# One output transfer per tile, a first tile of x by itself, and a new order of work

## The chip, the cores and the metric

The kernel runs on one core of a Trainium2 chip. The metric is the device time of one execution in microseconds (us); the median of three runs of the kernel before is 215.65 us (214.74 to 216.35). The core has five engines with an instruction stream each: PE (TensorE, matmuls; its weight loads are shown as PEld), DVE (VectorE), ACT (ScalarE), POOL (GpSimd) and SP (SyncE, which here only issues DMA transfers, in order). The transfers themselves are carried out by 16 DMA engines.

## The reference

For x of 2048 rows by 576 columns the result is the sum of three things:

```python
xn  = layernorm(x)                                  # over the 576 columns, eps 1e-5
A   = irfft2(rfft2(xn) * (w_r + 1j * w_i))          # over rows and columns
q   = einsum("nd,dhc->nhc", x, w_q)                 # 32 heads, c = 2 * 128
s1  = einsum("nhd,ed->nhe", q[..., :128], k1)       # 8 keys; s2 with k2
i1, i2 = argmax(s1), argmax(s2)                     # one of 8 each, top_e = 8 * i1 + i2
g   = softmax(one value) = 1
act = gelu(einsum("nd,nhd->nh", x, u[top_e]))       # tanh form
B   = einsum("nh,nhd->nd", g * act, v[top_e])       # 64 rows of u and v
out = x + A + B
```

## The kernel before

The rows are split into 16 tiles of 128. The work goes through five stages, which overlap.

1. Head. `ln` takes the mean and variance of each tile of x (DVE `BN_STATS` and `BN_AGGR`, or two ACT passes for the tiles in `SA`), and from them the factor `rr` of a row. `folds` adds and subtracts a tile's columns in mirrored pairs (`t`, then `F`, which the profile calls `A`), scales a 128x128 matrix by the rows' factors (`Rs`), and lays out the 33 middle columns (`yl`). `dft128` multiplies: two matmuls `Rs,yl` and four `Rs,A` per tile. The results of all 16 tiles go to `AB` and `ABL`. Statistics are done for groups of tiles: 2, 2, 4, 4 and 4, and the loads of x are cut the same way (`LOADS`).
2. Key fold. `fold_part` multiplies w_q (32 transfers of 576 KB) with the key differences `KP` (matmuls `w,KP`). These depend on no tile of x and are placed between other PE work.
3. Spectrum. For 16 groups g: `d_fwd` (matmuls `c,ABL` and `c,AB`; the first one needs all 16 tiles of the head), `s_fwd`, `s_mul`, `s_inv`.
4. Routing. `scores`, `route` and `combine` for 8 pairs of tiles.
5. Output. For each tile t, `d_inv(t)` and `fin(t, y)` (before: L1142). `fin` adds 16 matmuls of 64x64 weights into one PSUM pair, then one DVE `SCALAR_TENSOR_TENSOR` multiplies by a scale and adds x in place, into the tile `XN` (128 partitions by 2 by 288 columns: the partitions are 2 column halves c by 64 rows n, then 2 row halves h). Two transfers follow, one per column half:

```python
os = out.rearrange("(n h t) (c d) -> t c n h d", h=2, t=16, c=2)
for c in range(2):
    Q.dma_start(os[t, c], x[64 * c:64 * c + 64])
```

Each of the 32 transfers moves 144 KB from 64 partitions by 2 by 288 numbers to 128 rows by 288 numbers of the result in DRAM (the n and h steps merge into one step of 128): 128 pieces of 1152 bytes that are contiguous in DRAM.

Nothing is issued as it is written. A planner (`_Plan`) records every operation, gives it a cost (`cost`), merges runs of matmuls, and lays the operations out in time with a list of ranks (`RANK`, one number per operation) as priorities; instructions are then issued in that order on every engine. So each engine runs its stream in a fixed order that `RANK` and the costs determine, and waits for semaphores where data come from another engine. All recorded instructions have the line of the planner's loop (L542 before, L540 after). SP issues loads and outputs from one stream; all loads stand ahead of the outputs in it. The transfers use eight semaphores in turn, so a transfer waits until the eighth one before it has landed.

Of the kernel before, what the change touches and what calls it, by code (L numbers as in the profile page):

```python
# [14 lines left out]
AF = mybir.ActivationFunctionType  # L15
# [17 lines left out]
def _consts():  # L33
# [166 lines left out]
)  # L200
# [93 lines left out]
class _Plan:  # L294
# [41 lines left out]
    def add(self, eng, fn, m, args, kw):  # L336
# [7 lines left out]
        if AF.Gelu_apprx_tanh in args and not self.asked:  # L344
            self.asked, c = True, c + 1283.0
# [932 lines left out]
```

## Time and profile before

| | us |
|---|---|
| median of 3 runs | 215.65 (214.74 to 216.35) |
| profiled execution | 215.94, its span 214.2 |
| PE busy | 191.7 (89%) |
| DVE busy | 178.3 (83%) |
| ACT busy | 129.8 (61%) |
| POOL busy | 112.9 (53%) |
| mean granted TensorE clock | 0.987 |
| first matmul, last chain piece of PE until | 10.92, 208.13 |
| first output transfer issued | 180.81 |

The span runs from the first to the last instruction; the 1.7 us between the span and the profiled execution's own time lie around it. In the rows of the profile a group is named by what it writes and reads ("banks" is PSUM, `XN` the tiles of x and of the result, `out_dram` the result in DRAM). "us to landing" is from a transfer's issue to the moment its last data count as arrived. In rows on DMA, "share" is the busy time of packets as a share of 16 engines over the window; a packet is one contiguous piece.

### The profile page before, as it was taken

The numbers are of one execution on the slowest core, as the hardware profiler recorded it, in microseconds if no ns is written. First come the engines' busy times: TensorE is split into PE (matmuls) and PEld (weight loads), VectorE is DVE, ScalarE is ACT, GpSimd is POOL, SyncE is SP. The second block draws the span as 40 slices with busy tenths as digits, with TensorE's granted clock in tenths as the row PEclk, the third lists the DMA queues.
The fourth block names the chain that finished last, engine by engine and source line by source line (L and its number), as shares of the span: only waits on it lengthen the run. The fifth ranks groups of instructions, "written<-read, shape, count | busy, mean of one in ns | idle before, by whom it ended". The sixth has DMA issues, their size and how long they took to land.

```text
span 214.2 us, 6027 instructions
## 1 busy us (share of the span) xinstructions
PE 191.7 (89%) x2324; PEld 131.4 (61%) x2324; DVE 178.3 (83%) x426; ACT 129.8 (61%) x304; POOL 112.9 (53%) x153
## 2 busy tenths in 40 slices
PE   0093999989999999999999999999999999999980
PEld 0082877757856765674648464476465777878850
DVE  1999899941694956992999999999999999999880
ACT  2279699888948792984845964996454531222310
POOL 4356464612419840492523663879565147758750
PEclk9999799999999999999999999999999999999998
DMA  6999999999999999998543433102000000655566
GB/s 202 392 413 422 396 312 313 415 409 410 384 384 387 411 410 381 424 411 352 142 123 95 153 112 95 55 3 77 0 5 0 3 0 5 167 139 139 123 161 164
DMA packets 17020, 48.12 MB, mean 225 GB/s; under 512 B 2144, under 2 KB 8544, under 8 KB 16224
## 3 DMA queue, kind: packets, MB, share of 16 engines
q1 hardware_dynamic: 16992, 47.74, 62.7%
q8 instruction: 18, 0.29, 0.6%
q14 instruction: 10, 0.08, 0.1%
HBM read 43.01 MB, written 4.72 MB: 223 GB/s over the span
## 4 chain that ended last, share of the span: by engine, by line
PE 54%; DVE 32%; issue 5%; ACT 2%; POOL 2%; DMA 2%; DVEq 0%; POOLq 0%
PE banks L542 54%; DVE t L542 8%; DVE MT L542 5%; DVE A L542 4%; DVE st L542 3%; DVE w L542 2%; DVE AB L542 2%; DMA XN<-in_x_dram 2%; DVE ABL L542 2%; POOL t L542 2%; DVE mx L542 1%; DVE mm__96 L542 1%; DVE rr L542 1%; ACT yl L542 1%; POOL y L542 1%
## 5 line engine op out<-in xcount | busy, mean ns | idle before, releaser
L542 PE MATMUL banks<-MU,xT 128*128 128x512 f16 x192 | 45.2, 379 | 0.0
L542 PE MATMUL banks<-c,AB 128*128 128x145 f16 (+2 forms) x320 | 37.7, 251 | 0.4 <-DVE AB L542 0.4
L542 PEld LDWEIGHTS <-xT 128*128 128x128 f16 x224 | 20.9, 98 | 23.7 <-issue 0.4
L542 POOL TENSOR_TENSOR y<-t,t 128x289 f32<-128x289 f32 x32 | 23.2, 744 | 21.3 <-DVE t L542 19.1
L542 POOL TENSOR_TENSOR A<-t 128x289 f32<-128x289 f32 (+2 forms) x42 | 26.5, 649 | 14.7 <-PE banks L542 5.6
L542 DVE SCALAR_TENSOR_TENSOR t<-banks,wx,Wt 128x578 f32<-128x578 f32 x32 | 24.4, 811 | 4.4 <-ACT A L542 2.8
L542 POOL TENSOR_TENSOR yh<-y,yh 128x578 f16<-128x578 f32 x16 | 20.8, 1309 | 10.2 <-ACT yh L542 6.8
L542 PE MATMUL banks<-Rs,yl 128*99 128x128 f32 x64 | 11.2, 319 | 15.0 <-ACT yl L542 14.7
L542 POOL TENSOR_TENSOR xT<-xf,xT 128x640 f16<-128x640 f32 x10 | 14.2, 1428 | 17.8 <-ACT xf L542 11.0
L542 ACT ACTIVATE AB<-banks 128x512 f32<-128x512 f32 (+1 forms) x32 | 18.7, 591 | 3.8 <-PE banks L542 3.7
L542 PE MATMUL banks<-w,KP 128*32 128x288 f32 x256 | 20.3, 415 | 0.2 <-DMA w<-in_wq_dram 0.2
L542 ACT ACTIVATE yh<-banks 128x290 f32<-128x290 f32 (+1 forms) x16 | 7.3, 458 | 20.2 <-PE banks L542 13.5
L542 PEld LDWEIGHTS banks<-Rs,yl 128*99 128x99 f32 x64 | 9.0, 195 | 16.7 <-ACT yl L542 15.1
L542 PE MATMUL banks<-c,ABL 99*128 99x289 f16 (+1 forms) x64 | 19.1, 298 | 0.0
L542 POOL TENSOR_TENSOR t<-XN 128x289 f32<-128x289 f32 x14 | 13.1, 942 | 10.9 <-DVE A L542 5.3
L542 PEld LDWEIGHTS banks<-c,AB 128*128 128x128 f32 x128 | 18.0, 190 | 1.3 <-DVE AB L542 0.6
L542 PEld LDWEIGHTS banks<-Rs,A 128*128 128x128 f32 x128 | 16.7, 207 | 3.3 <-issue 2.3
L542 PE MATMUL banks<-Rs,A 128*128 128x128 f32 x128 | 18.3, 295 | 0.0
L542 DVE TENSOR_REDUCE MT<-w 128x128 bf16<-128x896 bf16 (+1 forms) x16 | 18.2, 1138 | 0.0
L542 PE MATMUL banks<-A,s 64*64 64x289 f32 x256 | 17.5, 410 | 0.0
L542 PEld LDWEIGHTS <-AB 128*128 128x128 f16 x192 | 17.2, 147 | 0.1
L542 DVE TENSOR_TENSOR ABL<-banks,ABL 33x256 f16<-33x256 f32 x32 | 13.0, 410 | 5.0 <-ACT ABL L542 4.7
(129 smaller groups left out, 408.4 us busy)
## 6 DMA issues: line engine op xcount, KB each, us to landing
w<-in_wq_dram SPq DMA_DIRECT2D x32, 576.0 KB, 6.9
xf<-in_xT_dram SPq DMA_DIRECT2D x16, 320.0 KB, 5.1
Wt<-in_W_dram SPq DMA_DIRECT2D x8, 578.0 KB, 6.6
out_dram<-XN SPq DMA_DIRECT2D x32, 144.0 KB, 2.5
XN<-in_x_dram SPq DMA_DIRECT2D x3, 1154.0 KB, 9.2
s<-in_s_dram SPq DMA_DIRECT2D x16, 192.0 KB, 4.4
XN<-in_xd_dram SPq DMA_DIRECT2D x2, 1152.0 KB, 9.0
XN<-in_xd_dram SPq DMA_DIRECT2D x1, 2304.0 KB, 10.6
```

Source lines behind the costliest of these rows:

```text
L542: ins = fn(*[x.place() if isinstance(x, _Ps) else x for x in args], **{k: x.place() if isinstance(x, _Ps) else x for k, x in kw.items()}).ins
```

## The change

Five things change.

- The first load of x covers tile 0 alone, the second tile 1, then tiles 2 and 3; the statistics are grouped 1, 1, 2, 4, 4 and 4.
- `fin` issues one transfer per tile, for both column halves. It moves 288 KB from 128 partitions by 2 by 288 numbers to 2 (column halves) by 128 (rows) by 288 numbers of DRAM.
- For tile 15, `fin` works on columns 0 to 143 and 144 to 287 of each half apart: 16 matmuls, one `SCALAR_TENSOR_TENSOR` and one transfer for each part, with 2 by 128 pieces of 576 bytes.
- Five costs or rules of the planner change (a factor for matmuls with 64x64 weights, POOL costs, the table load's cost, the rule for the port that DVE and POOL share, and the time for a change of the PE's tile shape).
- `RANK` is replaced, so the order on every engine is new.

```diff
-    464, 1220, 901, 1223, 1261, 1268, 1219, 1221, 391, 444, 431, 691, 894, 879, 874, 922, 835, 890, 883, 839,
...
+    1181, 1226, 1183, 1212, 1228, 1233, 1232, 1227, 1225, 897, 443, 1139, 442, 597, 1021, 564, 562, 563, 603,
...
-                return c * q[0] * q[1] / 16384 * (0.935 if q == [64, 128] else 1.065), 230.0
+                return c * q[0] * q[1] / 16384 * (0.935 if q == [64, 128] else 1.037), 230.0
...
-            return 45 + 1.15 * n, 75.0
+            return (45 if not ins else 120 if n > 16 else 200) + 1.15 * n, 75.0
...
-        if AF.Gelu_apprx_tanh in args and not self.asked:
+        if AF.Gelu_apprx_tanh in args and not self.asked and not self.extra:
...
-            len(sb) > 1 or m in ("tensor_copy", "tensor_scalar") and len(sb) == 1 == len(ins))
+            len(sb) > 1 or m in ("tensor_copy", "tensor_scalar") and len(sb) == 1)
...
-                    t0 = max(t0, free[e] + CHANGE)
+                    t0 = max(t0, free[e] + (120.0 if o.shape[0] == [128, 128] else 90.0))
...
-                if t0 - free[e] > 2500.0:
+                if t0 - free[e] > 2500.0 or not warm:
...
-    LOADS = ((0, 2), (2, 2), (4, 4), (8, 4), (12, 4))
-    Q.dma_start(XN[:, 0:2], xs[:, 0:2])
+    LOADS = ((0, 1), (1, 1), (2, 2), (4, 4), (8, 4), (12, 4))
+    Q.dma_start(XN[:, 0:1], xs[:, 0:1])
...
     def fin(t, y):
+        x = XD[:, t]
+        if t == 15:
+            for n, z in enumerate((slice(0, 144), slice(144, 288))):
+                p = PS("bc"[n])
+                for k in range(4):
+                    for h in range(2):
+                        hs = slice(64 * h, 64 * h + 64)
+                        for c in range(2):
+                            cs, ds = slice(64 * c, 64 * c + 64), slice(288 * c + z.start, 288 * c + z.stop)
+                            w, m = ((RT[hs], y[hs, ds]) if k == 0 else
+                                    (CAT[hs, t, 64 * (k // 3):64 * (k // 3) + 64], vS[hs, k % 2 ^ 1, ds]))
+                            P.matmul(p[cs, h, z], w, m, start=(k == 0), stop=(k == 3), tile_position=(64 * h, 64 * c))
+                V.scalar_tensor_tensor(x[:, :, z], p[:, :, z], sc[:, 11:12], x[:, :, z], op0=OP.mult, op1=OP.add)
+                Q.dma_start(os[t, :, :, :, z], x[:, :, z])
+            return
         p = PS("bc"[t % 2])
-        x = XD[:, t]
...
-        for c in range(2):
-            Q.dma_start(os[t, c], x[64 * c:64 * c + 64])
+        Q.dma_start(os[t], x)
...
-    for t, n in ((0, 2), (2, 2), (4, 4), (8, 4), (12, 4)):
+    for t, n in ((0, 1), (1, 1), (2, 2), (4, 4), (8, 4), (12, 4)):
         ln(t, n)
```

How the change moves instructions is shown at two places. The first is the end of SP's stream, the issue of the outputs. The numbers at a row's end are the shape that is written, slowest dimension first. Before:

```order
L542 DMA xf_126<-in_xT_dram 128x640
L542 DMA xf_124<-in_xT_dram 128x640
L542 DMA s_2_117<-in_s_dram 128x384
L542 DMA s_3_118<-in_s_dram 128x384
L542 DMA out_dram<-XN 128x1x288 x32
L1274 UNCONDITIONAL_BRANCH
```

After:

```order
L540 DMA xf_126<-in_xT_dram 128x640
L540 DMA xf_124<-in_xT_dram 128x640
L540 DMA s_2_117<-in_s_dram 128x384
L540 DMA s_3_118<-in_s_dram 128x384
L540 DMA out_dram<-XN 2x128x288 x15
L540 DMA out_dram<-XN 2x128x144 x2
L1285 UNCONDITIONAL_BRANCH
```

The last loads stand where they stood, ahead of all outputs. The outputs become 17 instead of 32, and the slowest dimension of what they write is 2 where it was 128.

The second place is on PE, the last matmuls of the head and the first of `d_fwd`. `Rs,yl` and `Rs,A` belong to `dft128`, `w,KP` to the key fold, and `LDWEIGHTS ABL` is the first instruction of `d_fwd`. Before:

```order
L542 MATMUL banks<-Rs_105,yl_107 99x2x8x8 x2
L542 MATMUL banks<-Rs_104,A_0_100 128x128 x4
L542 MATMUL banks<-w_120,KP 32x288 x4
L542 MATMUL banks<-w_122,KP 32x288 x4
L542 MATMUL banks<-Rs_105,A_3_103 128x128 x4
L542 MATMUL banks<-Rs_104,yl_106 99x2x8x8 x2
L542 MATMUL banks<-w_121,KP 32x288 x4
L542 MATMUL banks<-Rs_104,A_2_102 128x128 x4
L542 MATMUL banks<-w_119,KP 32x288 x4
L542 MATMUL banks<-w_123,KP 32x288 x4
L542 LDWEIGHTS ABL
```

After:

```order
L540 MATMUL banks<-Rs_105,A_3_103 128x128 x4
L540 MATMUL banks<-Rs_104,A_0_100 128x128 x4
L540 MATMUL banks<-w_121,KP 32x288 x4
L540 MATMUL banks<-w_120,KP 32x288 x4
L540 MATMUL banks<-w_123,KP 32x288 x4
L540 MATMUL banks<-Rs_104,yl_106 99x2x8x8 x2
L540 MATMUL banks<-Rs_104,A_2_102 128x128 x4
L540 MATMUL banks<-w_122,KP 32x288 x4
L540 LDWEIGHTS ABL
```

Between the last `Rs,yl` and `d_fwd`, three blocks of four `w,KP` matmuls stood before, and one stands after; ahead of the last `Rs,yl`, the key-fold blocks have moved forward. In all, 16 such blocks stand ahead of `d_fwd` before and 15 after. From the first matmul of `fin` on, PE has the same matmuls left in both orders, but for tile 15, whose 16 of 288 columns are 32 of 144.

124 rows, old and new, of the table RANK are left out of this document.

## The prediction

> **What bounds the kernel now.** I read the page first, then a table of stretches, the chain of waits, and last the transfers at the end.
>
> ```profile
> span 214.2 us, 6027 instructions
> PE 191.7 (89%) x2324; PEld 131.4 (61%) x2324; DVE 178.3 (83%) x426; ACT 129.8 (61%) x304; POOL 112.9 (53%) x153
> ...
> DMA  6999999999999999998543433102000000655566
> ...
> HBM read 43.01 MB, written 4.72 MB: 223 GB/s over the span
> ```
>
> PE is busy for 89% of the span. The DMA digits fall into two parts: loads for the first half, then little, then 5 to 6 tenths for the last 15%, where the 4.72 MB of output are written. Next, busy time by stretch; the columns are the stretch, its length, PE, PEld, DVE, ACT and POOL busy with instruction counts, the granted clock, the DMA share and GB/s.
>
> ```profile
> 4.59:10.92 6.33, 0.00 (x0) 0.00 (x1) 6.33 (x27) 1.66 (x5) 2.53 (x6) 1.00 1.01 381
> 10.92:21.16 10.24, 6.88 (x45) 5.86 (x45) 10.24 (x43) 8.57 (x25) 6.22 (x12) 0.99 1.02 422
> 21.16:25.50 4.34, 4.34 (x24) 4.23 (x24) 3.41 (x14) 2.70 (x8) 1.71 (x3) 0.63 1.03 425
> 25.50:45.00 19.50, 18.61 (x183) 13.50 (x183) 17.46 (x55) 17.65 (x52) 11.01 (x15) 1.00 0.95 350
> 45.00:51.95 6.95, 6.95 (x72) 4.72 (x72) 1.75 (x5) 6.15 (x13) 0.00 (x0) 1.00 1.03 413
> 51.95:90.00 38.05, 37.15 (x506) 25.50 (x503) 27.38 (x67) 28.82 (x58) 18.23 (x19) 1.00 1.02 396
> 90.00:178.00 88.00, 88.00 (x1008) 53.96 (x1008) 82.53 (x159) 55.32 (x125) 49.50 (x58) 1.00 0.31 104
> 178.00:208.20 30.20, 29.72 (x495) 23.64 (x493) 28.25 (x55) 7.61 (x22) 21.88 (x34) 1.00 0.53 125
> 208.20:214.20 6.00, 0.00 (x0) 0.00 (x0) 0.82 (x1) 0.00 (x0) 0.00 (x0) 0.82 0.70 168
> ```
>
> From 45.0 to 208.2 us PE stands still for only 0.90 + 0.48 = 1.4 us, so the bound there is PE's work. Ahead of that PE loses the time to 10.92 and then 10.24 - 6.88 = 3.4 and 19.50 - 18.61 = 0.9 us; there DVE is the busy engine. The last 6.0 us hold one DVE instruction and transfers. The chain of waits says the same (start, length, what):
>
> ```profile
> 0.72 3.85 DMA XN<-in_x_dram
> 4.59 1.54 DVE st L542 x4
> ...
> 44.58 0.38 ACT yl L542
> ...
> 45.00 17.48 PE banks L542 x182
> ...
> 89.86 54.45 PE banks L542 x560
> ...
> 178.47 29.66 PE banks L542 x493
> 208.22 0.82 DVE XN L542
> ```
>
> The end of the program lies behind the output transfers. The timeline has the first tile of the result, its first transfer, and the last two transfers; under them stand the transfers' own rows for the last 9 us:
>
> ```profile
> 179.98 0.80 DVE L542 SCALAR_TENSOR_TENSOR XN<-banks,sc,XN 128x576 f32<-128x576 f32 x1
> 180.81 0.63 SPq L542 DMA_DIRECT2D out_dram<-XN  x1
> 210.12 1.21 SPq L542 DMA_DIRECT2D out_dram<-XN  x2
> ```
> ```profile
> L542 SPq DMA_DIRECT2D out_dram<-XN x8: 528/582/617, 206.2 to 210.7; - x8
> ...
> DMA to landing us min/median/max: 2.4/2.4/2.5
> ```
>
> The 16 tiles come from DVE between 179.98 and 208.22 + 0.82 = 209.04, one per 1.8 us. The last tile's second transfer is issued at 210.7, because issues of 0.58 us stand in a row on SP; it lands 2.4 us later at 213.1, and the span ends 1.1 us after that.
>
> **The outputs, where the change decides.** A transfer is shared out among DMA engines, and the question is among how many. Four windows of the DMA rows give prices: the tail with outputs alone, the last 0.07 us in which any are left, one in which a single small packet remains, and a stretch of loads.
>
> ```profile
> DMA packets 871, 0.89 MB, mean 223 GB/s; under 512 B 98, under 2 KB 871, under 8 KB 871
> ...
> q1 hardware_dynamic: 871, 0.89, 92.8%
> ```
> ```profile
> DMA packets 7, 0.00 MB, mean 50 GB/s; under 512 B 4, under 2 KB 7, under 8 KB 7
> ...
> q1 hardware_dynamic: 7, 0.00, 16.9%
> ```
> ```profile
> DMA packets 1, 0.00 MB, mean 0 GB/s; under 512 B 1, under 2 KB 1, under 8 KB 1
> ...
> q1 hardware_dynamic: 1, 0.00, 0.2%
> ```
> ```profile
> DMA packets 856, 3.11 MB, mean 389 GB/s; under 512 B 96, under 2 KB 96, under 8 KB 855
> ...
> q1 hardware_dynamic: 855, 3.10, 100.4%
> ```
>
> The windows are 208 to 212, 212.73 to 212.8, 212.8 to 213.1 and 52 to 60 us. The first shows that now all 16 engines work on outputs: they are busy for 92.8%. It holds 871 - 98 = 773 pieces of 1152 bytes, and 0.928 x 16 x 4 us = 59.4 us of packet time. A small packet takes 0.002 x 16 x 0.3 us = 10 ns (third window), so a piece takes (59.4 - 1.0) / 773 = 76 ns with 16 engines at it. In the second window, with few left, three pieces and four small packets take 0.169 x 16 x 0.07 = 0.19 us, so a piece takes (0.19 - 0.04) / 3 = 50 ns. The loads move 3.10 MB in 1.004 x 16 x 8 = 128.5 us of packet time, 24.1 GB/s per engine, at which 1152 bytes take 48 ns: no engine has been seen faster.
>
> Up to now both sides of every output have a long slowest dimension: 64 partitions in SBUF, 128 rows in DRAM. The new transfer has 128 partitions on one side and 2 column halves on the other, as the order's last rows show. No transfer of the trace has a slowest dimension that short, so its spread is bounded from both sides: 16 engines, as in every row above, or 2, one per column half. I take 2, because cutting both address patterns at their slowest step is the one cut that needs no reordering of either, and 2 parts are all that it yields here.
>
> The Trainium skill, DMA: Bandwidth & Descriptors, section Why a DMA increments its semaphore by 16 and not by 1, states that rule outright: the number of engines is the largest one up to 16 that divides the slowest dimension (other than 1) of both sides. By it this transfer gets 2 engines, and the sum is the one made below; with all 16, the sum is that of the first rival. Every transfer of this trace divides by 16, so no run here shows it yet.
>
> The sum with two engines: a tile has 256 pieces, 128 per engine. 15 tiles at 50 ns are 15 x 128 x 0.050 = 96.0 us. Tile 15 has 512 pieces of 576 bytes, 256 per engine; with 10 ns fixed and half of the other 40 each takes 30 ns, 7.7 us. Together 103.7 us, which neither PE nor DVE hides: tiles arrive every 1.8 us and leave every 6.4 us, so the queue runs full from the second tile. SP then waits, with later outputs alone behind it, and no engine waits for SP, whose loads are all ahead. I take 50 ns since two engines have as little beside them as those in the second window; the upper bound is the 76 ns of 16 engines, with 576-byte pieces at 50: 15 x 128 x 0.076 + 256 x 0.050 = 158.7 us. The lower is 48 ns, and 24 for half a piece: 98.3 us.
>
> **What comes ahead of the outputs.** From the first `fin` on, the order leaves PE the same matmuls, so the first output moves as far as the work before it does.
>
> - First load: it holds half the bytes, 295 KB less. At the 381 GB/s of the first stretch that is 0.8 us; if the second load crowds in at once, nothing. I take 0.7. One `Sqrt` and one reciprocal more stand on ACT and DVE; by the order DVE has the same 142 instructions up to its last fold, so nothing is added there.
> - Head: three rows price the PE blocks around the start of `d_fwd`.
>
> ```profile
> 46.50 1.18 PE L542 MATMUL banks<-w,KP 128*32 128x288 f32 x16
> ...
> 48.61 0.60 PE L542 MATMUL banks<-Rs,yl 128*99 128x128 f32 x4
> ...
> 49.76 1.16 PE L542 MATMUL banks<-Rs,A 128*128 128x128 f32 x8
> ```
>
> Before, PE is still busy for 6.95 us from 45.0 until `d_fwd`, although the last `yl` came at 44.58. In the new order only 0.60 + 1.16 + 0.59 = 2.4 us of blocks stand from the last `Rs,yl` on, so 4.6 us could go forward, into the 3.4 + 0.9 us of idle time that PE has there. DVE, full in that stretch (10.24 of 10.24), may refuse it. One key-fold block (0.6 us) moves behind. Bounds 0 and 4.3; I take 1.8, so 2.5 us with the load.
> - Middle: PE's 1.4 us of idle time are the most that a better order can gain, and I allow as much loss. I take nothing.
>
> So the first output is issued at 180.8 - 2.5 = 178.3. A transfer's landing takes 2.4 us, of which 8 packets per engine at 76 ns are 0.6, so 1.8 are fixed. Span: 178.3 + 1.8 + 103.7 + 1.1 = 284.9. The profiled execution took 215.94, 1.7 more than its span, so the time is 286.6, say 287; against the median of 215.65, this execution was 0.3 us long, and I leave that.
>
> **Rivals.**
>
> 1. All 16 engines share each new transfer (it is cut along the list of its pieces, or along the 128). Then SP's queue at the end shortens: the last issue need not stand behind others. For it speaks that every transfer so far got 16 engines, and that 295 KB per 1.8 us, 162 GB/s, is less than the 223 GB/s of the tail. Tile 15 in two parts lets its last issue start right after DVE, near 209.6 in place of 210.7, but its pieces are shorter: 0.8 us gained, with 2.5 from the head. Time 215.9 - 3.3 = 212.6: faster. This is the case on the other side, and it decides by the number of engines k: a tile takes 256 / k x 50 to 76 ns, which stays under 1.8 us from k = 7 to 11 on. At 8 it would already be nearly as good as at 16.
> 2. 16 engines, but DVE, full from 4.59 to 21.16, takes the head's gain down to the load's 0.7 us, and an issue of 256 pieces takes twice the 0.58 us of one of 128, so that SP's queue is as long as before. Time 215.9 - 0.7 = 215.2: the same.
> 3. Two engines at the crowded price of 76 ns, if the price lies in the write itself and not in company: 178.3 + 1.8 + 158.7 + 1.1 + 1.7 = 341.6. This is the upper end of the forecast's own case.
>
> **How the numbers follow.** Two engines: 84 in 100, of which a fifth is the third rival. What speaks for it is the slowest dimension alone, which all rows so far leave open; 16 in 100 go to the other spread, 12 to the first rival and 4 to the second. The time is that of two engines at 50 ns, 287. Its range: below, 48 ns and a head that gains 4.3 + 0.8 us in place of 2.5, 175.7 + 1.8 + 98.3 + 1.1 + 1.7 = 278.6; above, 76 ns and no gain, 344.1. With 2 us for the middle's order, 276 to 346. That leaves out the 16 and little more. A measurement of this kernel tells about 1%, 2.2 us, from no change. Slower by over that: 0.84; faster: 0.12; within: 0.04.
>
> **What would show it.** The outputs' time to landing grows from 2.4 us to over 6 for the first and, with eight in flight, to some 50. The DMA digits of the slices after PE's end are 1 (2 of 16 engines), at some 45 GB/s. PE ends near 206, and its busy time stays near 191. If the outputs still land in about 2.5 us and the DMA digits stay at 5 to 9, the spread is wrong and with it the sign. If they land late but the rate is near 30 GB/s, the piece's price is wrong. If `d_fwd` begins at 51 or later, the head's term is.

## The result and the profile after

The changed kernel takes **288.78 us** (median of 6 runs, 287.79 to 289.37) against 215.94 us for the kernel before in the same session: a ratio of 1.338, 95% interval 1.333 to 1.344. It is 73 us slower, and the forecast was 287.

The profiled execution took 288.96 us. The page of after, with the same lines that were shown of before:

```profile
span 287.2 us, 6069 instructions
...
PE 192.1 (67%) x2344; PEld 130.8 (46%) x2344; DVE 178.5 (62%) x428; ACT 129.7 (45%) x305; POOL 110.2 (38%) x153
...
PE   0498799999999999999999999999900000000000
...
DMA  7999999999999953442011000011111111111111
...
HBM read 43.01 MB, written 4.72 MB: 166 GB/s over the span
```

PE, DVE and ACT are busy for as long as before (192.1 us against 191.7, 178.5 against 178.3, 129.7 against 129.8), POOL for 2.7 us less, and the same bytes are written. What has grown is the span. PE's digits end near three quarters of it (29 of 40 slices); from there on the DMA digit is 1 where it was 5 and 6. The stretches around the end (columns as before: stretch, length, PE, PEld, DVE, ACT and POOL busy, clock, DMA share, GB/s):

```profile
178.00:208.00 30.00, 29.39 (x514) 23.42 (x514) 27.98 (x57) 8.27 (x23) 22.98 (x36) 1.00 0.13 41
208.00:287.00 79.00, 0.67 (x36) 0.49 (x24) 1.13 (x3) 0.00 (x0) 0.00 (x0) 0.53 0.13 45
```

The DMA share is 0.13, which is 2 of 16 engines (0.125), at 41 to 45 GB/s. From 209.2 us on, where DVE ends, the program does nothing but wait for outputs. The transfers' own rows, on SP's timeline, in the table of issues (least, median and longest time of one issue in ns, then the first and the last issue), and in the DMA rows from 212 to 270 us:

```profile
180.82 1.51 SPq L540 DMA_DIRECT2D out_dram<-XN  x2
```
```profile
L540 SPq DMA_DIRECT2D out_dram<-XN x17: 669/6179/6661, 180.8 to 272.3; - x17
```
```profile
DMA packets 2365, 2.70 MB, mean 47 GB/s; under 512 B 18, under 2 KB 2365, under 8 KB 2365
...
q1 hardware_dynamic: 2365, 2.70, 13.6%
```

The first output is issued at 180.82 us, as in before (180.81). In 58 us the queue moves 2365 - 18 = 2347 pieces of 1152 bytes; two engines at work all the time make that 2 x 58 / 2347 = 49.4 ns a piece. This is a rate. By the share, the way in which 50 and 76 ns were read before, a piece takes (0.136 x 16 x 58 - 0.2) / 2347 = 53.7 ns: 13.6% is more than the 12.5% of two engines, so the times of successive packets seem to overlap a little. The 18 small packets stand at the ends of nine transfers, two for each. SP is held in each issue for 6.2 us, which is the time in which two engines write a tile (128 x 49.4 ns = 6.3 us).

### The profile page after: what moved, and what is told of

Its sections match the earlier page's. It is cut to its first block, busy times and chain, and to the rows that moved or that the text cites. A ratio compares the mean times of both kernels' runs of the same rounds, so it can differ in the third digit from the quotient of the medians.

```text
span 287.2 us, 6069 instructions
## 1 busy us (share of the span) xinstructions
PE 192.1 (67%) x2344; PEld 130.8 (46%) x2344; DVE 178.5 (62%) x428; ACT 129.7 (45%) x305; POOL 110.2 (38%) x153
## 4 chain that ended last, share of the span: by engine, by line
PE 37%; DVE 23%; ACT 6%; issue 4%; DMA 2%; POOL 1%; SPq 0%; POOLq 0%; DVEq 0%; ACTq 0%
PE banks L540 37%; DVE t L540 5%; DVE MT L540 5%; DVE w L540 3%; DMA XN<-in_x_dram 2%; DVE XN L540 2%; DVE A L540 1%; ACT t L540 1%; DVE st L540 1%; DVE AB L540 1%; ACT AB L540 1%; DVE mx L540 1%; DVE ABL L540 1%; POOL A L540 1%; ACT ABL L540 1%
## 5 line engine op out<-in xcount | busy, mean ns | idle before, releaser
L540 POOL TENSOR_TENSOR A<-t 128x287 f32<-128x287 f32 (+2 forms) x42 | 26.3, 644 | 10.3 <-DVE t L540 4.7
L540 PE MATMUL banks<-Rs,yl 128*99 128x128 f32 x64 | 12.1, 320 | 14.6 <-ACT Rs L540 12.6
L540 PE MATMUL banks<-w,KP 128*32 128x288 f32 x256 | 19.5, 413 | 0.0
L540 POOL TENSOR_TENSOR t<-XN 128x289 f32<-128x289 f32 x14 | 11.4, 822 | 12.0 <-DVE A L540 5.3
L540 ACT ACTIVATE xT<-xf,bx 128x640 f16<-128x640 f32 x16 | 13.2, 826 | 4.5 <-PE banks L540 4.5
```

The source lines that it names most:

```text
L540: ins = fn(*[x.place() if isinstance(x, _Ps) else x for x in args], **{k: x.place() if isinstance(x, _Ps) else x for k, x in kw.items()}).ins
```

## The experiments

Two questions were open: whether the spread over two engines is the whole loss, and why the head gave nothing. In all kernels below the planner's operations and their order are those of before or after; only what an operation of the planner issues is replaced (`calls`), unless the text says more.

**One transfer per tile, and nothing else.** The kernel before with

```diff
         for c in range(2):
             Q.dma_start(os[t, c], x[64 * c:64 * c + 64])
+        plan.ops[-2].calls = []
+        plan.ops[-1].calls = [(nc.sync.dma_start, (os[t], x), {})]
```

> The kernel before, in its own order, with one thing of the change alone: each tile of the result leaves in one transfer of 2 column halves x 128 partitions x 288 elements in place of two transfers. Theory (two DMA engines per such transfer, 50 ns a piece of 1152 bytes): first output at 180.8 as before, + 1.8 fixed + 16 x 128 x 0.050 = 102.4 + 1.1 to the span's end + 1.7 around the span = 288 us. Rival (the loss comes from the new order, the new loads or the halved last tile): 214 to 217 us, as before.

Measured: 287.90 us, ratio 1.335 (1.325 to 1.346). The one edit loses 71.9 us (against 216.01 in its session), where the whole change lost 72.8. So it is the cause by itself; what the rest of the change is worth lies hidden behind the outputs' queue here, and the run `a_two` below shows it.

**The same number of transfers, cut another way.** The kernel before with two transfers per tile by row half:

```diff
+        for h in range(2):
+            plan.ops[h - 2].calls = [(nc.sync.dma_start, (os[t, :, :, h], x[:, h]), {})]
```

> The kernel before, in its own order, still with two transfers of 128 pieces per tile, cut at the row halves in place of the column halves: on the DRAM side each is 2 column halves x 64 rows x 288, on the SBUF side 128 partitions x 288. Count, bytes, pieces and issues are those of before; only the slowest dimension of the DRAM side goes from 128 to 2. Theory (that dimension sets the number of engines, and it is always the same two): 288 us. Rival A (fewer, larger transfers are the cause): 214 to 217. Rival B (each transfer gets two engines, but two in flight get different pairs): 180.8 + 1.8 + 16 x 64 x 0.050 = 51.2 + 1.1 + 1.7 = 236.6 us.

Measured: 286.79 us, ratio 1.330 (1.317 to 1.343). Issues, bytes and pieces per transfer are those of before, and the loss is there. So it isn't the number or the size of the transfers (rival A falls). Two transfers in flight don't take different engines either (rival B falls): both of tile 0's are issued by 182.95 us, and from 183 to 188 us the rate is 45 GB/s, that of one pair of engines. All such transfers in flight share one pair.

**The slowest dimension from 4 to 16.** The kernel before with each column half's 128 rows walked as K by 128 / K, so that the rows of the result stand in another order. (The expectations call this 4 x 16, 8 x 8 and 16 x 4 rows; by the edit it is 4 x 32, 8 x 16 and 16 x 8. The slowest dimension is K in both.)

```diff
+    orow = out.rearrange("(r t) (c d) -> t c r d", t=16, c=2)
...
+        for c in range(2):
+            o = orow[t, c].rearrange("(b a) d -> a b d", a=4)
+            plan.ops[c - 2].calls = [(nc.sync.dma_start, (o, x[64 * c:64 * c + 64]), {})]
```

> The kernel before, in its own order, with its two transfers per tile by column half, but the DRAM side is walked as 4 x 16 rows: its slowest dimension is 4. (For that the 64 partitions of a half are written to permuted rows of the same tile, so the rows of the output stand in another order; bytes and pieces are the same.) Theory (as many engines as divide both slowest dimensions, here 4): a tile takes 256 / 4 x 0.050 = 3.2 us, more than the 1.8 us in which PE and DVE make one; 180.8 + 1.8 + 51.2 + 1.1 + 1.7 = 236.6 us, 263 at 76 ns a piece. Rival (only a slowest dimension of 2, or one that holds the column halves, is slow): 214 to 217.

> As the run with a slowest dimension of 4, but 8 x 8 rows (rows again permuted within their tile). Theory (8 engines): a tile takes 256 / 8 x 0.050 = 1.6 us, less than the 1.8 us in which one is made, so almost all of it hides: 216 to 218 us; at 76 ns a piece 2.4 us a tile, 224 us. The point from which the spread costs time lies between 4 and 8.

> As the runs with a slowest dimension of 4 and 8, but 16 x 4 rows (rows again permuted within their tile): the control for the permutation. Theory (16 engines): 214 to 217 us, as before. Rival (the scattered rows cost something themselves): over 218.

Measured: K = 4, 238.19 us, ratio 1.105 (1.096 to 1.113); K = 8, 219.73 us, 1.019 (1.010 to 1.028); K = 16, 215.99 us, 0.998 (0.995 to 1.001). The DMA rows from 208 to 212 us for K = 4, 8 and 16, in that order:

```profile
DMA packets 332, 0.37 MB, mean 93 GB/s; under 512 B 8, under 2 KB 332, under 8 KB 332
...
q1 hardware_dynamic: 332, 0.37, 27.2%
```
```profile
DMA packets 544, 0.59 MB, mean 147 GB/s; under 512 B 32, under 2 KB 544, under 8 KB 544
...
q1 hardware_dynamic: 544, 0.59, 48.3%
```
```profile
DMA packets 877, 0.90 MB, mean 225 GB/s; under 512 B 96, under 2 KB 877, under 8 KB 877
...
q1 hardware_dynamic: 877, 0.90, 71.1%
```

Four engines move 324 pieces in 4 us, 4 x 4 / 324 = 49.4 ns a piece, and the sum made with 50 (236.6) is within 1% of the time. With K = 8 the share is 48.3%, about eight engines of 16, and a piece takes (0.483 x 64 - 0.3) / 512 = 60 ns by the share. At 512 pieces in 4 us a tile needs 2.0 us and not the 1.6 expected. This is a little more than the 1.8 us in which one is made, in keeping with a time between the two that had been given for 50 and 76 ns. The control with 16 is as fast as before, so permuting the rows costs nothing.

The small packets count the spread without any share. The pages have them for the whole program: 2144 before and with K = 16, and with row halves, K = 4 and K = 8:

```profile
DMA packets 16572, 48.12 MB, mean 168 GB/s; under 512 B 1696, under 2 KB 8096, under 8 KB 15776
```
```profile
DMA packets 16636, 48.12 MB, mean 204 GB/s; under 512 B 1760, under 2 KB 8160, under 8 KB 15840
```
```profile
DMA packets 16764, 48.12 MB, mean 220 GB/s; under 512 B 1888, under 2 KB 8288, under 8 KB 15968
```

Only the 32 outputs differ between these programs: against before, each has 448 / 32 = 14, then 12 and 8 small packets fewer, and with K = 16 as many. The window of K = 16 has 96 of them for six transfers, which is 16 for each. So an output has 2 with row halves, and 4, 8 and 16 with K = 4, 8 and 16. This is one for each engine, as far as the shares tell the number of engines (13.6% for two, 27.2% for four and 48.3% for eight). The number of engines goes with the slowest dimension at 2, 4, 8 and 16.

This is the rule of the Trainium skill, DMA: Bandwidth & Descriptors, section Why a DMA increments its semaphore by 16 and not by 1: the largest number of engines up to 16 that divides the slowest dimension of both sides. All four sizes agree with it. The section also states that these transfers use the lowest-numbered engines; the run with row halves bears that out as far as it shows that transfers in flight share their two.

**The changed kernel with the column halves cut apart again.**

```diff
-        Q.dma_start(os[t], x)
+        Q.dma_start(os[t], x)
+        plan.ops[-1].calls = [(nc.sync.dma_start, (os[t, c], x[64 * c:64 * c + 64]), {}) for c in range(2)]
```

and the same for the two parts of tile 15.

> The changed kernel in its own order, with its loads and its halved last tile, but each part of the result leaves in two transfers by column half, as before (both slowest dimensions 64 or 128; the issues stand where the one stood). Theory (the spread over two engines is the whole loss, and the rest of the change is worth nothing, since the first output was issued at 180.82 against 180.81): 214.5 to 216.5 us, within 1% of before. Rival (the rest of the change loses too, or the spread doesn't explain all): over 218.

Measured: 217.48 us, ratio 1.0078 (1.0048 to 1.0109). The 73 us are gone, but 1.3 us above before remain, 1 us above the range expected. The trace's rows, for issues, for the first matmul of `d_fwd` and for DVE's end:

```profile
L540 SPq DMA_DIRECT2D out_dram<-XN x34: 528/603/1222, 180.7 to 212.4; - x34
```
```profile
50.83 0.30 PE L540 MATMUL banks<-c,ABL 99*128 99x289 f16 x1
```
```profile
208.15 0.95 DVE XN L540 x2
```

The first output (180.7 against 180.8) and DVE's end (209.10 against 209.04) are where they were. The last issue is at 212.4 against 210.7: tile 15 in two parts by two column halves makes 34 issues in place of 32, and SP's row of issues ends later. To test that, tile 15 is still computed in two parts but sent after the second, in two transfers:

> As the run with two transfers per part, with tile 15 still computed in two parts, but sent whole after the second: two transfers in place of four, 32 issues in place of 34. Theory (the 1.3 us by which that run is above before lie in SP's row of issues at the end, where its last one stood at 212.4 against 210.7): 1.2 us come back, 216.3. Rival (they lie in the head or the middle of the new order): stays at 217.5.

Measured: 216.60 us, ratio 1.0034 (1.0004 to 1.0064), in another session than `a_two`. Of the 1.3 us, 0.9 came back by the medians, but the two intervals overlap. The traces say more: from the first issue of an output to the last it is 29.9 us before, 31.7 in `a_two` and 30.4 here (182.7 to 213.1). So SP's row is longer with four transfers for tile 15; that it is most of the 1.3 us is likely, and not shown.

**The head.** The profile of after shows why its first load, half as large, gave nothing. DVE's timeline from 3.8 to 8.5 us, PE's first matmul, and the first two matmuls of `d_fwd`:

```profile
3.86 0.46 DVE L540 TENSOR_TENSOR t<-XN 128x289 f32<-128x289 f32 x1 [2.90 <-DMA XN<-in_x_dram]
...
5.74 0.46 DVE L540 BATCH_NORM_STATS2 st<-XN 128x6 f32<-128x288 f32 x1
7.61 0.46 DVE L540 BATCH_NORM_STATS2 st<-XN 128x6 f32<-128x288 f32 x1 [1.41 <-DMA XN<-in_x_dram]
7.99 0.45 DVE L540 TENSOR_TENSOR t<-XN 128x289 f32<-128x289 f32 x1
8.35 0.21 DVE L540 TENSOR_SCALAR rr<-rr 128x1 f32<-128x1 f32 x1
```
```profile
10.85 1.17 PE L540 MATMUL banks<-Rs,yl 128*99 128x128 f32 x4 [10.85 <-ACT Rs L540]
```
```profile
50.94 0.30 PE L540 MATMUL banks<-c,ABL 99*128 99x289 f16 x1
51.34 0.76 PE L540 MATMUL banks<-c,AB 128*128 128x145 f32 x4
```

Before, `d_fwd` began at 51.96:

```profile
51.96 0.30 PE L542 MATMUL banks<-c,ABL 99*128 99x289 f16 x1
```

Tile 0 arrives 0.7 us earlier (3.86 against 4.59), as forecast. But the new order puts a statistics instruction of tile 3 and the fold of tile 2, both from the third load, ahead of tile 0's scalars, and DVE waits 1.41 us for that load. The first matmul starts at 10.85, where it was 10.92. The experiment moves three instructions back, in the version with two transfers per part:

```diff
+        late = [64, 74, 76]
+        order = [i for i in order if i not in late]
+        k = order.index(36) + 1
+        order[k:k] = late
```

> As the run with two transfers per part, but three instructions stand later in the order: the statistics of tile 3's second half and the fold of tile 2 (both wait on the third load of x), and the POOL instruction that reads that fold, come behind tile 0's scalars and folds and tile 1's aggregate. Theory (DVE's wait of 1.41 us on that load, ahead of tile 0's scalars, is what ate the head's gain): the first matmul goes from 10.85 to about 8.6, and the time falls by 1.4 to 2.2 us against that run. Rival (DVE has the same work until 21 us in any order, and PE waits for it there): the first matmul comes earlier, the start of d_fwd stays at 51 and the time within 0.5 us.

Measured: 215.98 us, 1.50 us below the version without the move (217.48, same session); the ratio to before is 1.0019 (0.9990 to 1.0047). First matmul, the chain ahead of `d_fwd`, and the first matmul of `d_fwd`:

```profile
8.78 1.17 PE L546 MATMUL banks<-Rs,yl 128*99 128x128 f32 x4 [8.78 <-ACT Rs L546]
```
```profile
40.26 0.33 SPq L546
40.58 0.05 issue
40.63 9.73 DMA w<-in_wq_dram
50.37 0.04 issue
50.41 20.57 PE banks L546 x252
```
```profile
51.03 0.30 PE L546 MATMUL banks<-c,ABL 99*128 99x289 f16 x1
```

The first matmul comes 2.0 us earlier, and the gain of 1.5 us in the medians lies in the theory's 1.4 to 2.2; the rival's 0.5 falls. But the profiled execution doesn't show the gain at `d_fwd`: it starts at 51.03, against 50.83 without the move, as the rival had it. This execution took 216.91 us, one of the three longest of twelve. The chain shows what is late there: the key-fold block ahead of `d_fwd` waits for a load of `w`, which took 9.73 us. In the table of stretches of this run the DMA share is 0.99 and then 1.02:

```profile
25.00:45.00 20.00, 18.07 (x175) 13.57 (x176) 18.80 (x62) 18.70 (x55) 7.65 (x14) 1.00 0.99 364
45.00:52.00 7.00, 5.91 (x61) 3.81 (x60) 1.33 (x4) 6.47 (x11) 1.40 (x1) 1.00 1.02 392
```

The queue of loads is full, so an even earlier head would meet this load. In the run that has both the move and the second queue (`a_best` below) PE waits for no `w` there, and `d_fwd` starts 1.2 us earlier than without the move:

```profile
49.67 0.30 PE L546 MATMUL banks<-c,ABL 99*128 99x289 f16 x1
```

Its first output is issued at 179.6, against 180.7 in `a_two`. So the move gains where `w` is in time; that this is what the faster executions of `a_head` have in common is not shown, since one execution was profiled.

**The tail, and a version slightly below both.** Three runs issue the second column half of the last three tiles from ACT, whose last eviction lies before: the changed kernel with two transfers per part (`a_tail`), the same with the head's move (`a_best`), and that with tile 15 sent whole (`a_best2`). A fourth does it in the kernel before (`b_tail`):

```diff
+        if t > 12:
+            plan.ops[-1].calls = [(nc.scalar.dma_start, (os[t, 1], x[64:]), {})]
```

> As the run with two transfers per part, but the second column half of tiles 13 and 14 and of both parts of tile 15 is issued by ACT, which has nothing behind its last eviction there. Theory (SP's row of issues, some 0.58 us each, sets the end): the last issue starts near 209.3, and the time falls by 0.5 to 1.0 us. Rival (from 208 to 212 us 16 engines were busy for 92.8%: the bytes set the end): under 0.3 us.

> The three instructions later and the second halves at the end issued by ACT, both at once. If both theories hold, the two gains add up: 1.9 to 3.2 us below the run with two transfers per part, 212 to 214 us; if both rivals hold, the same as that run.

> The three instructions later, tile 15 sent whole, and the second column half of tiles 13 to 15 issued by ACT. From DVE's end the last transfer needs an issue of 0.6, a landing of 2.4 to 3.5 and 1.1 to the end; against the run that sends tile 15 in four pieces (215.65) this is between 0.5 less and 0.5 more. Both kernels are beaten by what can be measured only if it comes under 214.6.

> The kernel before, in its own order, with the second column half of tiles 13 to 15 issued by ACT. Theory (SP's row of issues sets the end; its last one stood at 210.7, DVE was done at 209.04): the last issues start near 209.4, 0.8 to 1.2 us less: 215 to 215.4. Rival (the bytes set the end): within 0.3 us of before.

| run | median us | ratio to before (95%) |
|---|---|---|
| a_tail | 217.23 | 1.0041 (1.0010 to 1.0072) |
| a_best | 215.65 | 0.9988 (0.9953 to 1.0022) |
| a_best2 | 215.10 | 0.9959 (0.9930 to 0.9989) |
| b_tail | 215.64 | 0.9971 (0.9946 to 0.9995) |

The second queue gains 0.25 us in the changed kernel, by the rival and within the noise, and 0.54 in the kernel before, between the theory and the rival. `a_best` misses the 212 to 214 expected if both theories held. The rows from 208 to 214 us, for `a_two` and `a_tail` (the last column is the time to landing in us), show one reason:

```profile
out_dram<-XN SPq DMA_DIRECT2D x4, 144.0 KB, 2.4
out_dram<-XN SPq DMA_DIRECT2D x4, 72.0 KB, 2.1
```
```profile
out_dram<-XN SPq DMA_DIRECT2D x2, 144.0 KB, 3.8
out_dram<-XN ACTq DMA_DIRECT2D x1, 144.0 KB, 3.9
out_dram<-XN ACTq DMA_DIRECT2D x2, 72.0 KB, 3.6
out_dram<-XN SPq DMA_DIRECT2D x2, 72.0 KB, 3.2
```

The issues come earlier, and each transfer takes 1.1 to 1.5 us longer to land, which gives most of the gain back. That the engines they share are the reason was not tested. The best version, 215.10 us, is 1.1 us under the 216.18 of before in its session. Much of that goes with the granted clock: where it was 0.992 or more the medians are 214.2 against 214.7, elsewhere 216.1 against 216.2, and six of its twelve executions but five of the 35 of before had the higher clock. Its interval leaves out 1, but it misses the 214.6 that had been set as the mark, and no more than 0.4% is claimed for it.

## Why the prediction was right

**Two engines: right.** The share of 0.13, the DMA digit 1 and 47 GB/s (forecast: some 45) are what was to show it, and the run with row halves and those with K = 4 to 16 show that the slowest dimension decides, by time, by share and by the count of small packets. The first rival (all 16 engines) falls, and with it the second.

**50 ns a piece: right, and in part by luck.** As a rate, which is what the sum needs, 49.4 was measured. The 50 had been read as a share of time, from three pieces; read in that way with two engines at work, a piece takes 53.7 ns, and 15 x 128 of them would be 103.1 us in place of 96.0. So an agreement within 1% is more than the reading could promise. The third rival, the crowded 76 ns on two engines (341.6 us), falls. The drain was put at 103.7 us; measured, from the first issue to the span's end less the fixed 1.8 and 1.1, it is 287.2 - 1.1 - 1.8 - 180.8 = 103.5.

**The head, 2.5 us gained: wrong, 0 measured at the first output.** At the first matmul of `d_fwd` 1.0 us is left (50.94 against 51.96); the second one then waits to 51.34 for an eviction of ACT (`AB`), and what is left is gone by 180.8. This is the step that failed, and it is nearly all of the difference between the span forecast (284.9) and measured (287.2). The 0.7 us of the load came. The 1.8 us "from 0 to 4.3", for which DVE was named as what might refuse, were refused by DVE in one place that the order showed and that was not weighed: the third load's instructions stand ahead of tile 0's scalars. The move of three instructions shows it: the first matmul comes 2.0 us earlier, and 1.50 us came back in the time. A second reason is seen in the trace alone and was not tested: from 43.2 to 51.3 us after's chain runs through ACT, which is busy for 6.97 of 7.00 us from 45 to 52.

```profile
45.00:52.00 7.00, 6.90 (x71) 5.04 (x70) 1.82 (x6) 6.97 (x16) 1.13 (x1) 1.00 1.01 391
```

The forecast's own test for this term was `d_fwd` at 51 or later; it began at 50.94, and went on from its second matmul at 51.34. The upper bound of 4.3 us was not reached with the head mended either: a load of `w` held `d_fwd` to 51.03 in one run, and in the other it began at 49.67, 2.3 us ahead of before.

**Middle 0: right within its margin.** It loses the 1.0 us between the start of `d_fwd` and the first output, of some 1.4 allowed; from one to the other it is 129.9 us after and 128.9 before, and 129.9 in `a_two` and in `a_best` too. PE's end was put near 206; in the table of stretches 0.67 us of its work still stand behind 208, which is the head's 2.5 us again.

**The time to landing, "some 50 us": not borne out.** The profile's rows give no landing for these transfers, but the two small packets at a transfer's end tell it: the first output's come at 189.4, 8.6 us after its issue (over 6, as forecast), the last ones at 285.8, 13.5 us after the issue at 272.3. The backlog isn't eight transfers on the queue, since SP is held 6.2 us in each issue. The sum doesn't use the 50.

**The first rival's side remarks.** At 8 engines the time was to be nearly as good as at 16: 219.73 against 215.99, 1.7% more, with 60 ns a piece. (The two were timed in different sessions, against 216.01 and 216.18 of before.) And that tile 15 in two parts gains at the end with 16 engines did not show: sent as four column-half transfers it was 0.9 us slower than sent whole, which the runs don't tell apart from nothing.

## What to carry to other kernels

Before two transfers are merged into one, write down both address patterns and look at the slowest dimension of each: here a merge that halved the issues turned the 128 of the DRAM side into 2, and with it 16 DMA engines into 2. Then compare (pieces per engine) x (time of one piece) with the time in which the data are made; here the spread cost nothing while that was shorter (16 engines), and the difference at every tile once it was longer (4 and 2). To see how many engines a transfer got, count the small packets at its end: here it was one for each. An earlier first load helps only if no instruction that waits for a later load stands ahead of the first tile's work in an engine's stream.

## What was not expected of the hardware

- SP is held inside an issue. With two engines, an issue of 256 pieces holds it for 6.2 us, and one of 128 pieces for 3.0 us, against 0.6 with 16 engines. Anything behind these issues in SP's stream, which runs in order, would have waited too. The row of the run with row halves:

```profile
L542 SPq DMA_DIRECT2D out_dram<-XN x32: 515/3024/3933, 181.1 to 272.3; - x32
```

- The time of one 1152-byte piece is not a constant of the engine. By the share it is 53.7 ns with 2 engines at work, (0.272 x 64 - 0.1) / 324 = 53 with 4, and 60 with 8. With 16 it was 76 ns in the kernel before and (0.711 x 64 - 1.0) / 781 = 57 ns in the control with 16 x 8 rows, at the same 223 to 225 GB/s. So the 76 ns, which the prediction took for a price of 16 engines, is not one that this rate needs; what sets it was not tested.
